# The sign word of the weight conversion: from a mask on VectorE to an add and a subtract on GpSimd

## The chip, the cores and the metric

The kernel runs on one core of a Trainium2 chip. The metric is the device time of one execution in microseconds (us); lower is better. The engines are named as in the profile: PE is TensorE (its weight loads are PEld), DVE is VectorE, ACT is ScalarE, POOL is GpSimd, SP issues most DMAs. Each engine works through its own list of instructions in order and waits for the others by semaphores.

## The reference

Eight batches of a two-way attention read are followed by a feed-forward block:

```python
def _attn_ref(x, state):              # x: 8 x 8 x 512 x 64, state: 8 x 8 x 32 x 64
    scores = scale * np.matmul(x, state.transpose(0, 1, 3, 2))
    a = softmax(scores); xread = np.matmul(a, state)
    scores2 = scale * np.matmul(state, x.transpose(0, 1, 3, 2))
    a2 = softmax(scores2); sread = np.matmul(a2, x)
    return np.concatenate([xread, sread], axis=2)

def _moe_ref(x, w_in, w_out):         # 4608 rows of 512; w_in 512 x 2048, w_out 2048 x 512
    h = x @ w_in
    g = h - np.tanh(h)
    return g @ w_out
```

(The softmaxes subtract the maximum and add 1e-9 to the sum.) `w_in` and `w_out` arrive as 8-byte numbers (float64), and the kernel makes 4-byte ones of them on the chip.

## The kernel before, in words

**Tiling.** The rows of the feed-forward block are cut into chunks: chunks 0 to 7 are the 512 x rows of one batch each, chunk 8 the state rows of all. `Chunk.hidden(f)` makes a 128 x 512 block of `h` in PSUM (tile `hps`), `Chunk.finish` (L523) takes tanh of it on ACT (tile `t`), subtracts on DVE, and splits the result into a high part (a cast on ACT) and a low part (a subtraction on DVE); `split` at L104 to L106 does this for every operand, so L106 is both a cast on ACT and a TENSOR_TENSOR on DVE. `Chunk.output(f)` multiplies the parts with the split rows of `w_out` (tiles `wo`) into `ops`. A product of two split operands is three matmuls (L515 to L517, L575 to L577). A batch's attention (`attention`, L313) leaves the tile `aT` (its two halves split at L393), which the chunk's first `hidden` needs.

**Weight conversion.** `Weight.steps` turns one 128 x 512 block of 8-byte numbers (tile `raw`, named `w..d` or `wo..d`) into 4-byte ones in four steps: L138 shifts the high words left by 3 and masks off two bits; L139 masks sign and top exponent bit out of the topmost 16-bit word into every second 16-bit element of a tile `r` (names `w..r`, `wo..r`, pool tag `c2` with four buffers); L140 on ACT scales the low words into the other elements; L141 adds the two as integers. There are 32 such blocks: `w00` to `w33` of `w_in`, `wo0` to `wo15` of `w_out`. A row of `w_out` is then split into `wo` by L106.

**Stages.** A start-up written out by hand (`SEQ`, L802) converts `w00` to `w03`, `wo0`, `wo1`, computes batch 0's attention and the first hidden blocks; in it, `a` to `p` with a number are the four conversion steps of a block. Then chunk 0's first eight blocks, chunk 1, the rest of chunk 0, chunks 2 and 3, and two pairs of chunks (class `Pair`) follow; the conversions of the other 26 blocks lie in chunk 0 and the first half of chunk 1, ahead of about 105 us.

**What sets the order.** Outside `SEQ` the instructions of each engine are put in order when the program is built: a scheduler goes by its own estimates of durations, by priorities and by `issue_after` gates. `convert` (L144) returns one step's instruction to such gates (`turn`), so that a conversion is issued behind the one before. The order is then fixed: an engine that waits at an instruction does nothing of what stands behind it. `m_first_two` (L163) multiplies converted `w_in` blocks by the state (PSUM tiles `mps`, L187); `free` (L202) copies these on ACT (L207).

Of the kernel before, what the change touches and what calls it, by code (L numbers as in the profile page):

```python
# [13 lines left out]
U16 = mybir.dt.uint16  # L14
ALU = mybir.AluOpType
# [16 lines left out]
LONE = 1  # L32
HALT = 8
PLAIN = (0, 1, 7)
TURN = ((0, 1, 2, 3), (1, 0, 3, 2))


@with_exitstack
def attention_ffn(ctx: ExitStack, tc: tile.TileContext, xT, xn, bd, bh, sp, sm, sl, win, wout, xout, tout, sout):
# [10 lines left out]
    nc = tc.nc  # L50
# [57 lines left out]
    class Weight:  # L108
# [17 lines left out]
        def steps(self, dst):  # L126

            if self.src.dtype == F32:
                return [lambda: None] * 3 + [lambda: nc.gpsimd.tensor_copy(dst, self.raw)]
            low, high = self.raw[:, :, 0], self.raw[:, :, 1]  # L130
            u, i = dst.bitcast(U32), dst.bitcast(I32)


            r = pool.tile([P, 512, 2], U16, tag="c2", name=f"{self.name}r", bufs=CSB)
            rest, top = r[:, :, 0], r[:, :, 1]
            return [

                lambda: nc.vector.tensor_scalar(u, high, 3, 0x3FFFFFFF, ALU.logical_shift_left, ALU.bitwise_and),  # L138
                lambda: nc.vector.tensor_single_scalar(top, self.raw.bitcast(U16)[:, :, 3], 0xC000, ALU.bitwise_and),  # L139
                lambda: nc.scalar.activation(rest, low, AF.Copy, scale=2.0**-29),  # L140
                lambda: nc.vector.tensor_add(i, i, r.rearrange("p f w -> p (f w)").bitcast(I32)),  # L141
            ]

        def convert(self, dst):  # L144
            return [step() for step in self.steps(dst)][1].ins


    m_first = {}
# [147 lines left out]
    def convert_wout(f, part):  # L296
        if f in PLAIN:
            if f // 2 not in plain:
                plain[f // 2] = big(f"wp{f}", [P, 2, DM], F32)
            return part.convert(plain[f // 2][:, f % 2])  # L300
        w = pool.tile([P, 512], F32, tag="c2", name=f"wor{f}", bufs=CSB)
        made = part.convert(w)
        wo[f] = big(f"wo{f}", [P, 2, DM], F32R)
        low = split(wo[f][:, 0], wo[f][:, 1], w)[1].ins
        return low if f in (2, 3) else made
# [7 lines left out]
    def attention(b, aT):  # L313
# [22 lines left out]
        def all_scores():  # L336
# [3 lines left out]
            for j in (2, 0, 3, 1):  # L340
                at = TURN[b][j] if b < 2 else j
                for hf in (1, 0):
# [68 lines left out]
    def state_read(b, ss):  # L411
# [40 lines left out]
        for hf in range(2):  # L452
            for k in range(4):
                for c in range(4):
                    cs = slice(32 * c, 32 * c + 32)
                    j = TURN[b][c] if b < 2 else c
                    with ExitStack() as behind:
# [11 lines left out]
        for hf in range(2):  # L469
            for j in range(4):  # L470
                h = 4 * hf + (TURN[b][j] if b < 2 else j)
                js = slice(32 * j, 32 * j + 32)
# [18 lines left out]
    class Chunk:  # L491
# [31 lines left out]
        def finish(self, f, ps):  # L523
            i, n = self.i, self.n
            t = pool.tile([P, 512], F32, tag="t", name=f"t{i}_{f}", bufs=TB)[:, :n]
            if CL <= i < B:
# [4 lines left out]
                return  # L531
            if i == 0 and f in PLAIN:
                g = self.g[f] = pool.tile([P, 512], F32, tag="g", name=f"g{i}_{f}", bufs=GB)
# [33 lines left out]
        def add(self, f, t):  # L567
            g, o = self.g[f], self.o[t]
            tok = slice(t * P, t * P + P)
            stop = f + 1 in self.begins or f == NFF - 1 or (self.i == B and t == 1 and f == NFF - 3)  # L570
            if self.i == 0 and f in PLAIN:
                w = plain[f // 2][:, f % 2]
# [81 lines left out]
    SPLITS = [8,9,10]  # L654
    split_it = iter(PLAIN)
    PAIRS = [1, 1, 9, 9, 11, 11, 13, 13, 15, 15]
# [556 lines left out]
```

## Time and profile before

| | |
|---|---|
| median of 3 runs | 637.64 us (637.53 to 640.27) |
| span of the profiled execution | 635.4 us (2.2 us less than the median) |
| PE busy | 627.7 us, 99% of the span |
| DVE busy | 474.8 us, 75% |
| ACT busy | 380.3 us, 60% |
| POOL busy | 24.0 us, 4%, nearly all of it DMA issue after 527 us |
| granted PE clock | 1.00, that is 2.4 GHz, in every stretch shown |

The page gives the profiled execution's time as its span alone; what a run takes beyond it lies around the kernel. PE's busy time includes the modelled tails of its matmuls, so it doesn't show by itself that PE always works; the start times of the matmuls do (three of a split product start 0.23 us apart, one of two 4-byte operands takes 0.86 us).

### The profile page before, as it was taken

What the parts mean: (1) busy time and instruction counts of PE and PEld (TensorE: products, weight loads), DVE (VectorE), ACT (ScalarE), POOL (GpSimd) and SP (SyncE); (2) the same over time, 40 slices, a digit from 0 to 9 for tenths busy, and PEclk for the clock granted to TensorE, in tenths of its full rate; (3) what the DMA queues carried; (4) which work ended last, traced back from release to release, by engine and by line L of the source; (5) the groups of instructions that cost most, each with busy time, mean ns of one, the idle gap of its engine ahead of it and who ended that gap; (6) DMA issues with size and microseconds to landing.
All of it is one profiled execution on the core that took longest, in us unless ns stands there. A gap on an engine that the chain in (4) does not pass through costs nothing.

```text
span 635.4 us, 9664 instructions
## 1 busy us (share of the span) xinstructions
PE 627.7 (99%) x3490; PEld 489.2 (77%) x3490; DVE 474.8 (75%) x770; ACT 380.3 (60%) x656; POOL 24.0 (4%) x38
## 2 busy tenths in 40 slices
PE   7999999999999999999999999999999999999997
PEld 4456677777777788778888788788888888888996
DVE  5999997686667956999445889989955789754542
ACT  5777777567666757676554675637565554533432
POOL 0000000000000000000000000000000001233200
PEclk9999999999999999999999999999999999999999
DMA  9993866568879856679952644765555537999700
GB/s 319 361 387 132 297 226 183 187 190 254 261 239 294 271 198 219 217 268 346 364 189 87 206 144 141 230 226 163 169 178 181 172 100 239 299 338 329 252 1 33
DMA packets 67439, 141.21 MB, mean 222 GB/s; under 512 B 6976, under 2 KB 28736, under 8 KB 67392
## 3 DMA queue, kind: packets, MB, share of 16 engines
q1 hardware_dynamic: 64544, 131.95, 63.4%
q0 software_dynamic: 2560, 8.39, 4.0%
q8 instruction: 27, 0.44, 0.3%
q10 hardware_dynamic: 288, 0.26, 0.1%
q14 instruction: 20, 0.16, 0.1%
HBM read 96.01 MB, written 44.56 MB: 221 GB/s over the span
## 4 chain that ended last, share of the span: by engine, by line
PE 94%; DVE 3%; ACT 2%; DMA 1%; issue 0%; ACTq 0%
PE X L1048 14%; PE hps L515 10%; PE hps L516 10%; PE hps L517 10%; PE ops L575 10%; PE ops L576 9%; PE ops L577 9%; PE Y0m L1048 5%; PE Y1m L1048 5%; PE mps L242 2%; PE mls L249 2%; PE ops L573 2%; PE rps L461 1%; PE pps L440 1%; PE hps L789 1%; PE mps L187 1%
## 5 line engine op out<-in xcount | busy, mean ns | idle before, releaser
L575 PE MATMUL ops<-wo,g 128*128 128x512 f32 x244 | 96.2, 400 | 0.0
L576 PE MATMUL ops<-wo,g 128*128 128x512 f32 x244 | 95.5, 391 | 0.0
L515 PE MATMUL hps<-aT,m 128*128 128x512 f32 x240 | 94.4, 395 | 0.0
L516 PE MATMUL hps<-aT,m 128*128 128x512 f32 x240 | 93.8, 391 | 0.1
L517 PE MATMUL hps<-aT,m 128*128 128x512 f32 x240 | 93.4, 390 | 0.0
L577 PE MATMUL ops<-wo,g 128*128 128x512 f32 x244 | 88.4, 396 | 0.0
L536 DVE TENSOR_TENSOR t<-hps,t 128x512 f32<-128x512 f32 (+1 forms) x77 | 48.7, 633 | 45.2 <-ACT t L536 44.8
L530 ACT ACTIVATE t<-hps 128x512 f32<-128x512 f32 x64 | 38.4, 599 | 66.3 <-PE hps L517 66.0
L536 ACT ACTIVATE t<-hps 128x512 f32<-128x512 f32 (+1 forms) x77 | 42.5, 552 | 56.7 <-PE hps L517 56.1
L530 DVE TENSOR_TENSOR G<-hps,t 128x512 f32<-128x512 f32 x64 | 43.9, 687 | 28.9 <-ACT t L530 28.7
L106 DVE TENSOR_TENSOR g<-t,g 128x512 fp32r<-128x512 f32 (+1 forms) x77 | 48.5, 632 | 16.1 <-ACT g L106 15.2
L575 PEld LDWEIGHTS ops<-wo,g 128*128 128x128 f32 x244 | 45.6, 188 | 17.4 <-ACT t L536 2.3
L106 ACT CAST g<-t 128x512 fp32r<-128x512 f32 (+1 forms) x77 | 44.3, 576 | 23.2 <-DVE t L536 22.8
L577 PEld LDWEIGHTS ops<-wo,g 128*128 128x128 f32 x244 | 45.5, 188 | 12.6 <-issue 2.5
L515 PEld LDWEIGHTS hps<-aT,m 128*128 128x128 f32 x240 | 45.1, 188 | 12.4 <-issue 2.0
L576 PEld LDWEIGHTS ops<-wo,g 128*128 128x128 f32 x244 | 45.8, 188 | 10.5 <-issue 1.1
L516 PEld LDWEIGHTS hps<-aT,m 128*128 128x128 f32 x240 | 45.1, 188 | 9.9 <-DVE aT L106 0.5
L517 PEld LDWEIGHTS hps<-aT,m 128*128 128x128 f32 x240 | 45.0, 188 | 9.4
L1048 PE MATMUL X<-g0m,W0m 128*128 128x512 f32 x192 | 47.8, 389 | 0.0
L1048 PE MATMUL X<-g1m,W1m 128*128 128x512 f32 x192 | 45.8, 389 | 0.0
L106 ACT CAST g1m<-G 128x1024 fp32r<-128x1024 f32 x28 | 29.2, 1054 | 27.0 <-PE X L1048 9.9
L1086 POOL DMA_DIRECT2D wl<-wod x32 | 23.3, 728 | 574.2 <-DMA wn<-wf 526.6
(275 smaller groups left out, 1134.5 us busy)
## 6 DMA issues: line engine op xcount, KB each, us to landing
mr<-md SPq DMA_DIRECT2D x26, 512.0 KB, 4.3
xT<-in_xT SPq DMA_DIRECT2D x16, 512.0 KB, 6.1
md<-st SPq DMA_DIRECT2D x64, 128.0 KB, 3.1
xn<-in_xn SPq DMA_DIRECT2D x16, 512.0 KB, 5.6
wsd<-ws SPq DMA_DIRECT2D x16, 512.0 KB, 4.7
wod<-wo SPq DMA_DIRECT2D x32, 256.0 KB, 7.3
W0m<-wsd SPq DMA_DIRECT2D x16, 512.0 KB, 3.6
W1m<-wsd SPq DMA_DIRECT2D x16, 512.0 KB, 4.7
```

The costliest lines, as they stand in the source:

```text
L106: return nc.scalar.copy(hi, src), (sub or nc.vector).tensor_sub(lo, src, hi)
L242: made = nc.tensor.matmul(pss[e], s0[rows, x, 2 * p + e], t[rows, y], start=(n == 0), stop=(n == 2))
L515: nc.tensor.matmul(ps, mhi[k][:, cols], ahi[:, k], start=(k == 0), stop=False)
L516: nc.tensor.matmul(ps, mhi[k][:, cols], alo[:, k], start=False, stop=False)
L517: made = nc.tensor.matmul(ps, mlo[k][:, cols], ahi[:, k], start=False, stop=(k == nk - 1))
L530: main(nc.scalar.activation(t, ps, AF.Tanh), nc.vector.tensor_sub(g, ps, t))
L536: tanhs.append((nc.scalar.activation(t, ps, AF.Tanh).ins, nc.vector.tensor_sub(t, ps, t).ins))
L575: nc.tensor.matmul(o, g[:, 0, tok], w[:, 0], start=(f in self.begins), stop=False)
L576: nc.tensor.matmul(o, g[:, 0, tok], w[:, 1], start=False, stop=False)
L577: return nc.tensor.matmul(o, g[:, 1, tok], w[:, 0], start=False, stop=stop).ins
L1048: made = nc.tensor.matmul(out[t], w[:, e, x, cols], y[:, e], start=first and j == 0 and e == 0 and c == 0, stop=last and j == 3 and e == 1 ...
L1086: nc.gpsimd.dma_start(wo[f][:, :, cols].bitcast(F32), wod[:, f % 2, half, f // 2])
```

## The change

The mask step leaves DVE. GpSimd reads the same 16-bit words, adds 1.5 * 2^37 to each and subtracts it again, which rounds the word to a multiple of 2^14, and writes it as 16 bits. The shift on DVE loses its mask: the two bits it leaves cancel in the integer add against the rounded word. `convert` now returns the shift, which is the first step, since the second is no longer on DVE.

```diff
@@ -32,6 +32,7 @@
 PLAIN = (0, 1, 7)
+COARSE = 1.5 * 2.0**37
 TURN = ((0, 1, 2, 3), (1, 0, 3, 2))
@@ -135,14 +136,14 @@
             return [
-                lambda: nc.vector.tensor_scalar(u, high, 3, 0x3FFFFFFF, ALU.logical_shift_left, ALU.bitwise_and),
-                lambda: nc.vector.tensor_single_scalar(top, self.raw.bitcast(U16)[:, :, 3], 0xC000, ALU.bitwise_and),
+                lambda: nc.vector.tensor_single_scalar(u, high, 3, ALU.logical_shift_left),
+                lambda: nc.gpsimd.tensor_scalar(top, self.raw.bitcast(U16)[:, :, 3], COARSE, COARSE, ALU.add, ALU.subtract),
                 lambda: nc.scalar.activation(rest, low, AF.Copy, scale=2.0**-29),
                 lambda: nc.vector.tensor_add(i, i, r.rearrange("p f w -> p (f w)").bitcast(I32)),
             ]
         def convert(self, dst):
-            return [step() for step in self.steps(dst)][1].ins
+            return [step() for step in self.steps(dst)][0].ins
```

Every line of the changed kernel behind L34 has a number higher by one. The scheduler, which knows other estimates for POOL than for DVE, also puts other instructions in another order. Two places matter below. The first is ACT's list where row 3 of `w_out` is split (`wor_404` is the converted row, `wo_410` its split; `mps_388` and `mps_389` are the second pair of state products). Before:

```order
L140 ACTIVATE wo3r<-wo3d 128x512
L207 COPY mr_312<-mps_322 128x512
L106 CAST m_561<-mr_187 128x1024
L207 COPY mr_313<-mps_323 128x512
L106 CAST wo_410<-wor_404 128x512
L140 ACTIVATE wo4r<-wo4d 128x512
L140 ACTIVATE wo5r<-wo5d 128x512
L207 COPY mr_312<-mps_388 128x512
```

And now:

```order
L208 COPY mr_312<-mps_322 128x512
L107 CAST m_561<-mr_187 128x1024
L141 ACTIVATE wo3r<-wo3d 128x512
L208 COPY mr_313<-mps_323 128x512
L208 COPY mr_312<-mps_388 128x512
L208 COPY mr_313<-mps_389 128x512
L107 CAST wo_410<-wor_404 128x512
L537 ACTIVATE t_4_418<-hps_4_415 128x512
```

The cast of `wo_410` has moved behind the copies of `mps_388` and `mps_389`. The second place is DVE's list from the low part of that split on. Before:

```order
L106 TENSOR_TENSOR wo_410<-wor_404,wo_410 128x512
L138 TENSOR_SCALAR wor_461<-wo4d 128x512
L139 TENSOR_SCALAR wo4r<-wo4d 128x512
L138 TENSOR_SCALAR wor_502<-wo5d 128x512
L139 TENSOR_SCALAR wo5r<-wo5d 128x512
L141 ISA wor_461<-wor_461,wo4r 128x1024
L141 ISA wor_502<-wor_502,wo5r 128x1024
L138 TENSOR_SCALAR wor_543<-wo6d 128x512
L139 TENSOR_SCALAR wo6r<-wo6d 128x512
L106 TENSOR_TENSOR wo_467<-wor_461,wo_467 128x512
L106 TENSOR_TENSOR wo_508<-wor_502,wo_508 128x512
```

And now:

```order
L107 TENSOR_TENSOR wo_410<-wor_404,wo_410 128x512
L139 TENSOR_SCALAR wor_461<-wo4d 128x512
L139 TENSOR_SCALAR wor_502<-wo5d 128x512
L537 TENSOR_TENSOR t_4_418<-hps_4_415,t_4_418 128x512
L537 TENSOR_TENSOR t_5_475<-hps_5_472,t_5_475 128x512
L107 TENSOR_TENSOR g_4_421<-t_4_418,g_4_421 128x512
L142 ISA wor_461<-wor_461,wo4r 128x1024
L376 STREAM_TRANSPOSE e_437<-s_434 128x512
L376 STREAM_TRANSPOSE e_443<-s_434 128x512
L139 TENSOR_SCALAR wor_543<-wo6d 128x512
```

The masks are gone, and the sums and splits of rows 4 and 5 now stand among the work on `t_4`, `t_5` and the attention of batch 1. From the low part of `wo_410` to the low part of `aT`'s first half, DVE's list holds the same instructions in both but for the masks of `wo4` to `wo7`.

## Rows read from the trace of the kernel before

**Rows 1.** Page: span, then busy us, share of span and instructions
```profile
span 635.4 us, 9664 instructions
...
PE 627.7 (99%) x3490; PEld 489.2 (77%) x3490; DVE 474.8 (75%) x770; ACT 380.3 (60%) x656; POOL 24.0 (4%) x38
```
**Rows 2.** Windows: stretch, us, busy of each engine (instructions), clock, DMA
```profile
19.09:105.00 85.91, 85.83 (x406) 54.96 (x406) 84.45 (x164) 65.34 (x112) 0.00 (x0) 1.00 0.75 266
35.08:54.62 19.54, 19.54 (x95) 11.86 (x94) 19.50 (x41) 12.94 (x23) 0.00 (x0) 1.00 0.71 271
105.00:635.40 530.40, 526.96 (x3002) 425.13 (x2998) 378.41 (x581) 303.50 (x524) 23.29 (x32) 1.00 0.66 211
```
**Rows 3.** Waits of PE: for whom, us in total, times, longest
```profile
PE mps L773 <- DVE w L141: 1.5, 2, 0.9
PE warm L701 <- DVE blank L73: 1.2, 1, 1.2
PE tps L716 <- ACT s L710: 0.8, 1, 0.8
PE aps L739 <- DVE e L734: 0.4, 1, 0.4
PE sps L705 <- DMA bdr<-in_bd: 0.2, 1, 0.2
```
**Rows 4.** Windows of L139 alone on DVE: stretch, us, busy (instructions)
```profile
0.00:110.00 110.00, 14.72 (x32) 1.00 0.78 275
35.08:54.62 19.54, 1.90 (x4) 1.00 0.71 271
...
20.00:55.00 35.00, 4.67 (x10) 1.00 0.82 305
55.00:110.00 55.00, 7.44 (x16) 1.00 0.70 234
```
**Rows 5.** Timeline, DVE: start, duration, instruction; back to back
```profile
30.45 0.47 DVE L139 TENSOR_SCALAR w12r<-w12d 128x512 uint16<-128x512 uint16 x1
30.79 0.42 DVE L138 TENSOR_SCALAR w<-w13d 128x512 uint32<-128x512 uint32 x1
31.12 0.46 DVE L139 TENSOR_SCALAR w13r<-w13d 128x512 uint16<-128x512 uint16 x1
...
47.38 0.70 DVE L378 TENSOR_TENSOR e<-e,m 128x512 f32<-128x512 f32 x1
47.98 0.70 DVE L536 TENSOR_TENSOR t<-hps,t 128x512 f32<-128x512 f32 x1
```
**Rows 6.** Timeline of the start-up: start, duration, instruction [idle before]
```profile
6.49 0.46 DVE L139 TENSOR_SCALAR w00r<-w00d 128x512 uint16<-128x512 uint16 x1 [5.35 <-DMA w00d<-in_win]
...
9.07 0.68 DVE L141 CUSTOM_DVE_ANT_0 w<-w,w00r 128x1024 uint16<-128x1024 uint16 x1
...
12.11 1.09 PE L773 MATMUL mps<-w,sps 128*64 128x128 f32 x16 [0.61 <-DVE w L141]
...
12.98 0.78 ACT L140 ACTIVATE w03r<-w03d 128x512 uint16<-128x512 uint32 x1 [0.70 <-DMA w03d<-in_win]
```
**Rows 7.** Timeline, 34 to 42 us: the split of row 3 and the copies
```profile
34.07 0.62 ACT L106 CAST wo<-wor 128x512 fp32r<-128x512 f32 x1 [0.49 <-DVE wor L141]
...
35.08 0.70 DVE L106 TENSOR_TENSOR wo<-wor,wo 128x512 fp32r<-128x512 f32 x1
...
36.11 1.09 PE L187 MATMUL mps<-w,sps 64*32 64x512 f32 x16
...
37.24 0.59 ACT L207 COPY mr<-mps 128x512 f32<-128x512 f32 x1 [0.64 <-PE mps L187]
...
37.77 1.22 ACT L106 CAST wo<-wor 128x512 fp32r<-128x512 f32 x2
...
39.37 0.79 ACT L140 ACTIVATE wo6r<-wo6d 128x512 uint16<-128x512 uint32 x1
40.02 0.79 ACT L140 ACTIVATE wo7r<-wo7d 128x512 uint16<-128x512 uint32 x1
```
**Rows 8.** Timeline, 54 to 56 us: aT's low part and PE
```profile
54.62 1.46 DVE L106 TENSOR_TENSOR aT<-at,aT 128x512 fp32r<-128x512 f32 x2
...
54.62 0.61 PE L515 MATMUL hps<-aT,m 128*128 128x512 f32 x2
55.32 0.50 PE L516 MATMUL hps<-aT,m 128*128 128x512 f32 x1
```
**Rows 9.** Groups of POOL instructions: busy, mean ns, idle before
```profile
masks.py:199 POOL TENSOR_SCALAR_AFFINE_SELECT ident<-ident 128x128 f32<-128x128 f32 x1 | 0.3, 287 | 0.1
masks.py:197 POOL MEMSET ident<- 128x128 f32 x1 | 0.2, 204 | 0.3 <-POOLq L1198 0.3
...
L1198 POOL MEMSET const-float32-0.0<- 128x1 f32 x1 | 0.1, 93 | 0.2 <-issue 0.2
```

## The prediction

> **What bounds the kernel now.** I read the page's busy shares first: PE is busy for 627.7 of 635.4 us [rows 1]. Since a busy PE need not be a fed one, I looked at stretches next: from 19.09 us to 105 us it lacks 0.08 us of 85.91, and from 105 us on 3.4 us of 530.4 [rows 2]. PE's own waits add up to 4.1 us, and all of them lie in the start-up, before 19 us [rows 3]. So from 19 us on the kernel is one stream of matmuls, at full clock. Nothing that makes another engine faster can shorten that stream. A change can win only what PE waits in the start-up, and it loses whatever time PE is newly left without work.
>
> DVE is the other engine to watch: until 105 us it is busy for 84.45 of 85.91 us [rows 2], so PE is fed just in time. Where it is closest shows at 55 us: chunk 1's first matmuls with the high part of `aT` start at 54.62, 0.23 us apart, the next needs the low part, which DVE makes from 54.62 to 55.31, and it starts at 55.32 [rows 8]. PE has nothing else to do there. The path to the end runs through DVE's making of `aT`, without slack.
>
> **What leaves DVE, and what that is worth.** There are 32 masks, all before 110 us [rows 4]. Back to back, a mask starts 0.34 us before the next instruction [rows 5], so DVE loses 32 x 0.335 = 10.7 us of work. The shift keeps its price: the same one instruction with one operation fewer, and 0.335 us is what mask and shift, with one and two operations, both take.
>
> In the start-up, two PE waits can shrink. The second `mps` product waits 0.61 us for a conversion [rows 6], with one mask ahead of its sum that goes: -0.335. The transposes `aps` wait 0.4 us [rows 3] behind a second mask: at most -0.37 more. Not all of it arrives, since ACT has to copy `aps` and stands at `w03r` until that block lands at 12.98 [rows 6]. I take -0.5 us, with 0 and -0.7 as ends. The other 26 masks bring nothing by themselves, because PE doesn't wait there. On SP the stores of converted blocks and the loads for batches 1 and 2 change places in nine lines; the only DMA that PE waits for is the first, 0.2 us [rows 3], so I cost this at nothing; the cover is that the loads are issued well ahead of their use.
>
> **What is added on POOL.** POOL does nothing in this stretch [rows 2]. Its trace shows no instruction like the new one, so I bound it. A memset takes 93 ns for one column and 204 ns for 128, the select, which reads and writes, 287 ns [rows 9]; stretched in a straight line to 512 columns that is an estimate of 0.54 us and 0.87 us. The new one reads and writes like the select, but builds no pattern: I take 0.7 us, between the two. The queue holds 32 x 0.7 = 22 us in 100. In the start-up the word of `w00` is due at 9.07 and can start at 6.49 [rows 6], 2.6 us for an instruction of 0.7: hidden under DVE's other work. Cover would be gone above 2.6 us each. POOL's DMAs all come after 105 us [rows 2], behind the last new instruction.
>
> **What moves: a new wait at row 3 of `w_out`.** This is the term that I expect to decide the sign. Before, ACT's cast of `wo_410` starts at 34.07 and DVE's low part at 35.08 [rows 7], while the product pair `mps_388`, `mps_389` runs on PE only at 36.11 and its first copy on ACT at 37.24 [rows 7]. In the new order ACT makes this cast behind both copies. PE gets to the pair by its stream, 0.5 us earlier by the start-up's gain. So: first copy at 37.24 - 0.5 = 36.74; copies and casts follow at 0.53 us (37.24 to 37.77), so the second copy starts at 37.27 and the cast at 37.80; it takes 0.62 and ends at 38.42. DVE's low part, due in its list, waits for it, idle, and starts at 38.45 rather than 35.08. Queued behind it on DVE is everything up to `aT`.
>
> Between these two points DVE worked 19.54 us without a pause (19.50 busy) [rows 2]. The list is the same but for four masks [rows 4], 1.34 us: 18.2 us. One more wait appears: DVE reaches `g_4`'s low part after the low part, two shifts and two 0.60 us subtractions [rows 5], at 38.45 + 0.6 + 0.67 + 1.2 = 40.92, but ACT has, from 38.33, two tanh (0.5 each), two conversions (0.65 each, 39.37 to 40.02 [rows 7]) and the cast (0.62): 41.25. That is 0.3 us. `aT`'s low part then starts at 38.45 + 18.2 + 0.3 = 57.0, where it started at 54.62 [rows 8]: +2.4 us, all on PE, since its stream has no other work. The four masks and the start-up's 0.5 us are inside this sum.
>
> **The price of POOL beside DVE.** The masks of `wo5`, `wo6`, `wo7`, `w20`, `w21` run on POOL in that stretch, while DVE is the path. If the two engines don't disturb each other this costs 0. If DVE had to stand still during each, it costs 5 x 0.7 = 3.5 us (5 x 0.87 = 4.4 at the long end). No row shows the two at once on tiles in SBUF. I take a middle value: in 18.2 us DVE has four shifts (1.34 us) and 15 instructions of 0.60 us with both operands in SBUF (splits, integer sums, the subtraction and scaling of `e`), 10.3 us or 57%; if those alone exclude POOL, five instructions cost 0.57 x 3.5 = 2.0 us. After 57 us there are 14 more; DVE is relieved of 16 masks [rows 4], 5.4 us, there, and delayed by at most 14 x 0.7 x 0.57 = 5.6: nothing, with +4.4 as the end (14 x 0.7 - 5.4).
>
> The Trainium skill speaks against the change here: SBUF — State Buffer, section "SBUF: two separate sides", says that VectorE and GpSimd share one pair of ports, held exclusively for a whole instruction, and that a VectorE instruction with two SBUF inputs collides with a GpSimd one that reads SBUF. No row of this kernel shows it; by that rule the 2.0 us fall due, without it the sum stops at +2.4. GPSIMD Engine Reference, section "Engine selection", calls one-input work on GpSimd roughly line-rate: an estimate of 512 / 1.2 GHz = 0.43 us for an instruction, which would make the same term 1.2 us.
>
> **Sum.** +2.4 (new wait, net of all gains) + 2.0 (POOL beside DVE) = +4.4 on the profiled execution's 635.4 us, so 639.8; with the 2.2 us by which the runs' median stands above this span, 642.0 us.
>
> **Rivals.** *The order alone.* POOL doesn't hinder DVE: +2.4, 640.0 us. For it: nothing in the trace shows a collision. Against: most of what DVE does there reads two tiles of SBUF.
>
> *Not slower.* DVE gets its 3.35 us (the ten masks between 20 and 55 us [rows 4]) and `aT` comes no later than PE asks for it; the start-up's gain stays: -0.5, 637.1 us. The mechanism is that ACT doesn't stand at the copies: if the pair of products came to PE 2.4 us or more earlier than at 36.11, the cast would be done by 36 and the saved masks would cover the rest. For it: DVE is the path there and loses work. Against: PE's stream before the pair has no gap [rows 2], so the pair can't come earlier than the start-up allows.
>
> *POOL heavier.* 0.87 us an instruction, DVE standing still for each: 2.4 + 4.4 = 6.8, and after 57 us DVE falls behind by 14 x 0.87 - 5.4 = 6.8 us, of which I let a third reach PE, 2.2: +9.0, 646.6 us. For it: DVE has no spare time until 105 us. Against: such a price needs both ends at once.
>
> That the change doesn't do what it says I leave out; the masks are gone from DVE's list.
>
> **How the numbers follow.** Chances: forecast 0.42, with a range of its own of 640.6 to 643.8; order alone 0.27; not slower 0.13; POOL heavier 0.18. The range for 8 in 10 goes from 638.2, just above the third case, to 646.5: what is left out is most of that case and the upper half of the last. About 0.5%, 3.2 us, is what a measurement here can tell from no change. Above 640.8 lie nearly all of the forecast (0.40), a little of the order alone (0.03) and the heavy case (0.17): slower 0.60. Within: 0.37. Faster by 3.2 us isn't in reach, as the start-up holds 4.1 us of waits and the change touches 1.0 of them [rows 3]: 0.03 for error.
>
> **What would show it.** In the profile after: POOL with 32 TENSOR_SCALAR of 0.5 to 0.9 us; DVE idle for about 3 us ahead of a split of `wo` at 35 to 38 us, released by ACT; PE with a wait of 2 us or more for `aT` near 57 us, where no wait was; no PE wait to speak of after 110 us. The port term shows as longer spacing than 0.60 us, or idle time without a releaser, on DVE between 38 and 58 us: 2 us in all if right, none if the rival is. I am wrong if `aT` comes by 55 us, if PE waits elsewhere (at `wo4` to `wo6` for instance) for longer than for `aT`, or if the start-up gets longer because POOL's words come late.

## The result, and the profile after

The changed kernel takes 642.98 us (median of 6 runs, 642.09 to 645.06), the kernel before 637.39 us beside it: a ratio of 1.0085, with a 95% interval of 1.0071 to 1.0098. It is 5.6 us slower; 642.0 us had been forecast. The profiled execution has a span of 641.1 us, 5.7 more than before [rows 1]. The page's span, then busy us, share and instructions:

```profile
span 641.1 us, 9713 instructions
...
PE 628.9 (98%) x3490; PEld 489.3 (76%) x3490; DVE 473.5 (74%) x738; ACT 380.3 (59%) x656; POOL 98.2 (15%) x70
```

DVE has 32 instructions fewer but is hardly less busy: 1.3 us less, where 10.7 us of masks went. POOL gained 32 instructions and 74 us, that is 2.3 us each. PE's waits (for whom, us in total, times, longest):

```profile
PE mps L774 <- DVE w L142: 2.8, 2, 1.8
PE hps L516 <- ACT aT L107: 1.5, 1, 1.5
...
PE ops L577 <- DVE wo L107: 0.9, 1, 0.9
...
PE hps L514 <- ACT mr L208: 0.7, 1, 0.7
PE mps L765 <- DVE w L142: 0.5, 1, 0.5
```

Against [rows 3], the wait for `mps` has grown by 1.3 us, one of 0.5 is new and the 0.4 us for `aps` is gone: that is the start-up. The other three are new and lie between 39 and 61 us. All of PE's waits add up to 8.8 us, where they were 4.1; PE's busy time, which counts the modelled tails of the matmuls, has grown by 1.2 us with the same 3490 matmuls. The start-up, in order of time (start, duration, instruction, idle time before it and what ended it):

```profile
6.66 2.34 POOL L140 TENSOR_SCALAR w00r<-w00d 128x512 uint16<-128x512 uint16 x1 [5.35 <-DMA w00d<-in_win]
...
10.13 2.14 POOL L140 TENSOR_SCALAR w01r<-w01d 128x512 uint16<-128x512 uint16 x1 [1.13 <-DMA w01d<-in_win]
...
12.19 2.27 POOL L140 TENSOR_SCALAR w02r<-w02d 128x512 uint16<-128x512 uint16 x1
12.31 1.09 DVE L142 CUSTOM_DVE_ANT_0 w<-w,w01r 128x1024 uint16<-128x1024 uint16 x1 [1.11 <-POOL w01r L140]
...
13.45 1.09 PE L774 MATMUL mps<-w,sps 128*64 128x128 f32 x16 [1.78 <-DVE w L142]
```

Before, the sum of `w01` stood here:

```profile
11.36 0.69 DVE L141 CUSTOM_DVE_ANT_0 w<-w,w01r 128x1024 uint16<-128x1024 uint16 x1
```

POOL begins the word of `w01` when the block lands, at 10.13, and takes 2.14 us. DVE waits 1.11 us for it, and the sum itself, which begins just behind the start of POOL's next word, takes 1.09 us where before a sum took 0.68 [rows 6]. The second product starts at 13.45 instead of 12.11 [rows 6], 1.34 us later: 0.95 for the late start of the sum (12.31 and 11.36), 0.4 for its length.

The place at row 3 of `w_out`:

```profile
36.16 1.88 PE L514 MATMUL hps<-at,mr 128*128 128x512 f32 x4
...
37.97 1.09 PE L188 MATMUL mps<-w,sps 64*32 64x512 f32 x16
39.10 1.07 ACT L208 COPY mr<-mps 128x512 f32<-128x512 f32 x2 [3.05 <-PE mps L188]
...
40.06 0.63 ACT L107 CAST wo<-wor 128x512 fp32r<-128x512 f32 x1
...
40.73 0.69 DVE L107 TENSOR_TENSOR wo<-wor,wo 128x512 fp32r<-128x512 f32 x1 [3.33 <-ACT wo L107]
```

Here stands what the prediction said: ACT waits 3.05 us for PE's pair of products, copies both tiles, and only then makes the cast, so DVE stands idle for 3.33 us. The matmul at 36.16 is the one that stood at 34.30 [rows 7]; it and the pair (36.11 before) are both 1.86 us late, which is what the start-up lost in these two profiles. Then `aT`, and the stretches of DVE's way to it and of the rest (columns as in [rows 2]):

```profile
60.34 1.29 DVE L107 TENSOR_TENSOR aT<-at,aT 128x512 fp32r<-128x512 f32 x2
60.36 0.73 PE L516 MATMUL hps<-aT,m 128*128 128x512 f32 x2 [1.49 <-ACT aT L107]
...
63.49 3.59 PE L574 MATMUL ops<-wp,g 128*128 128x512 f32 x8
```
```profile
40.73:60.34 19.61, 17.19 (x75) 10.56 (x73) 19.43 (x36) 12.73 (x23) 13.02 (x6) 1.00 0.54 183
...
110.00:641.10 531.10, 527.37 (x3004) 425.41 (x3002) 379.08 (x583) 303.74 (x524) 23.40 (x32) 1.00 0.65 212
```

DVE's low part of `aT` starts at 60.34 instead of 54.62 [rows 8], 5.72 us late, and the end is 5.7 us late: after `aT` nothing is lost or won in sum. DVE needs 19.61 us for the same way that took 19.54 [rows 2], though four masks of 1.34 us are gone. So the 5.72 us are 1.86 (start-up), 3.79 (row 3: low part at 40.73 where 35.08 + 1.86 = 36.94 would have kept pace) and 0.07 (the way to `aT`).

### The profile page after: what moved, and what is told of

The parts are those of the page before. It is cut to its first block, busy times and chain, and to the rows that moved or that the text cites. A ratio compares the mean times of both kernels' runs of the same rounds, so it can differ in the third digit from the quotient of the medians.

```text
span 641.1 us, 9713 instructions
## 1 busy us (share of the span) xinstructions
PE 628.9 (98%) x3490; PEld 489.3 (76%) x3490; DVE 473.5 (74%) x738; ACT 380.3 (59%) x656; POOL 98.2 (15%) x70
## 4 chain that ended last, share of the span: by engine, by line
PE 91%; DVE 3%; DMA 2%; ACT 1%; POOL 1%; issue 1%; SPq 0%; ACTq 0%
PE X L1049 14%; PE hps L516 10%; PE hps L517 10%; PE hps L518 10%; PE ops L576 9%; PE ops L578 9%; PE ops L577 9%; PE Y0m L1049 5%; PE Y1m L1049 5%; PE mps L243 2%; PE mls L250 2%; PE ops L574 2%; DMA w01d<-in_win 1%; PE rps L462 1%; PE hps L790 1%; PE pps L441 1%
```

## The experiments

The three causes are the six words of the start-up on POOL, the other 26 on POOL, and the late cast at row 3. They were switched one by one; the scheduler still moves other instructions when a part of the words is on POOL, so that a run can change more than its one cause (start_dve below). Who makes a word is chosen by the block's name:

```diff
+            self.pool = name not in ('w00', 'w01', 'w02', 'w03', 'wo0', 'wo1')
...
-                lambda: nc.gpsimd.tensor_scalar(top, ...
+                (lambda: nc.gpsimd.tensor_scalar(top, ...)) if self.pool
+                else (lambda: nc.vector.tensor_single_scalar(top, ..., 0xC000, ALU.bitwise_and)),
```

(the shift keeps its mask wherever DVE makes the word). With either part on DVE the scheduler puts row 3's cast ahead of the copies again; where it was to stay late, the cast and the low part of row 3 were gated:

```diff
+        with ExitStack() as behind:
+            if f == 3:
+                behind.enter_context(tc.issue_after(freed[0]))
-        low = split(wo[f][:, 0], wo[f][:, 1], w)[1].ins
+            low = split(wo[f][:, 0], wo[f][:, 1], w)[1].ins
```

Single profiles differ by up to 1.1 us in the start-up even where nothing in it was changed, so the last two columns read each trace from one point on: the start of the `hps` matmul that stood at 34.30 us before [rows 7], and the time from there to DVE's low part of `aT`. The start-up's differences begin ahead of the conversion: DVE's sum of `w00` starts at 9.07 us before, at 9.25 in the change, and between 8.93 and 9.88 in the kernels that make this block's word on DVE.

| kernel | start-up words | other 26 | cast of row 3 | median / before, us | ratio, 95% interval | `hps` at | to `aT` |
|---|---|---|---|---|---|---|---|
| before | DVE | DVE | early | | | 34.30 | 20.32 |
| start_pool | POOL | DVE | early | 638.99 / 637.72 | 1.0021 [1.0010, 1.0032] | 35.93 | 20.46 |
| start_dve | DVE | POOL | early | 639.19 / 637.72 | 1.0024 [1.0007, 1.0041] | 34.79 | 22.09 |
| cast_late | DVE | DVE | late | 642.30 / 637.72 | 1.0071 [1.0053, 1.0089] | 34.83 | 24.13 |
| start_dve_late | DVE | POOL | late | 641.53 / 637.29 | 1.0069 [1.0057, 1.0082] | 35.39 | 24.15 |
| start_pool_late | POOL | DVE | late | 644.63 / 637.29 | 1.0117 [1.0103, 1.0131] | 36.65 | 24.14 |
| changed | POOL | POOL | late | 642.98 / 637.39 | 1.0085 [1.0071, 1.0098] | 36.16 | 24.18 |

**start_pool.** 

> Only the six blocks of the start-up have their word made by POOL; the other 26 keep mask and masked shift on DVE, and ACT's and DVE's lists at row 3 are those of before. Theory: the words of w01 and w02 come late, since an instruction takes 2.1 us and can't start before the block lands, and PE waits for the two sums: first hidden matmul at 36.2 us where before had 34.30, and nothing is given back, since PE's stream has no gap after it: +1.9 us, 639.3 us (638.8 to 639.8). Rival (the start-up's loss comes from the order or is made up while DVE has slack up to 28 us): within 0.5 us of before, 637.4. Rival (the prediction's step): -0.5 us, 636.9.

PE's second product and the `hps` matmul:

```profile
13.42 1.09 PE L779 MATMUL mps<-w,sps 128*64 128x128 f32 x16 [1.44 <-DVE w L147]
...
35.93 1.88 PE L519 MATMUL hps<-at,mr 128*128 128x512 f32 x4
```

The same late product as in the change, and the loss reaches the `hps` matmul, 1.6 us late; from there to `aT` it goes as before (20.46). About 0.5 of the 1.6 us were there already at the sum of `w00`, at 9.56 instead of 9.07, which waited for no word. The runs say 1.3 us (0.0021 x 637.5, interval 0.6 to 2.0). The start-up's loss is real and nothing gives it back; the prediction's gain of 0.5 us falls.

**start_dve.** 

> The six blocks of the written-out start-up (w00 to w03, wo0, wo1) keep the mask and the masked shift on DVE; the other 26 words are made by POOL as in the change. The scheduler then puts ACT's cast of row 3 of w_out ahead of the second pair's copies again, as in the kernel before. Theory (the change's 5.7 us are 1.9 us of late words in the start-up, about 2.7 us of the wait at row 3, about 1.2 us of POOL beside DVE): the first hidden matmul is back at 34.3 us (36.16 with the whole change), DVE's low part of row 3 at about 35.1 us without idle time of 3 us ahead of it, and of the 1.2 us most is paid by the four masks that DVE is rid of on the way to aT: 0 to +1 us against before, 638.0 us (637.2 to 638.6). Rival 1 (words of 2.05 us are late all along, the start-up is not special): +3 us or more, 640.5. Rival 2 (POOL beside DVE costs the 2.0 us or more that the prediction took, and the masks pay none of it): +2 us, 639.4.

DVE's timeline:

```profile
30.89 1.00 DVE L140 TENSOR_SCALAR w<-w13d 128x512 uint32<-128x512 uint32 x1
31.82 0.86 DVE L140 TENSOR_SCALAR wor<-wo3d 128x512 uint32<-128x512 uint32 x1
...
33.80 1.21 DVE L107 TENSOR_TENSOR m<-mr,m 128x1024 fp32r<-128x1024 f32 x1
34.93 1.13 DVE L147 CUSTOM_DVE_ANT_0 wor<-wor,wo3r 128x1024 uint16<-128x1024 uint16 x1
36.75 0.69 DVE L107 TENSOR_TENSOR wo<-wor,wo 128x512 fp32r<-128x512 f32 x1 [0.68 <-ACT wo L107]
```

The idle time of 3 us is gone and the time is still 1.5 us above before (0.4 to 2.6). I had 0 to 1 us; the second rival's 2 us is as near. DVE's instructions are longer here and there: shifts of 1.00 and 0.86 us where before one took 0.42 [rows 5], a sum of 1.13 instead of 0.68. But the 1.77 us that the way from the `hps` matmul to `aT` is longer are not POOL's collisions alone. DVE's low part of row 3 starts 1.96 us behind the `hps` matmul instead of 0.78: in this list the low part of `m` (33.80) stands ahead of the sum of row 3 (34.93) and no longer behind it, so that ACT's cast comes late and DVE waits 0.68 us. From there to `aT` DVE takes 20.13 us for what took 19.54, with four masks fewer. So with POOL beside DVE more is lost than the masks bring, in part by collisions and in part by the changed order; this run does not separate the two.

**cast_late.** 

> The kernel before with all masks on DVE and nothing on POOL; only the cast and the low part of row 3 of w_out are issued behind the copies of the second pair of state products, as the change's order has them, and DVE's list behind it has the subtraction on t_4 ahead of the sums, much as in the change. Theory (the order at row 3 by itself costs what DVE waits there): first copy at 37.24 us as before, cast at 38.3, DVE's low part at 38.9 after some 3 us of idle time, then 19.5 us of work: aT's low part at 58 to 58.8 us where before had 54.62, so +3.2 to +4.2 us, 641.1 us. That is more than the 2.7 us that I put down to it in the change, since here DVE keeps its four masks. Rival (DVE catches up, or PE has other work until aT comes): +1 us or less, 638.4. The start-up stays: first hidden matmul at 34.3 us.

ACT and DVE, in order of time:

```profile
37.76 1.07 ACT L207 COPY mr<-mps 128x512 f32<-128x512 f32 x2 [3.66 <-PE mps L187]
38.72 0.63 ACT L106 CAST wo<-wor 128x512 fp32r<-128x512 f32 x1
...
39.38 0.69 DVE L106 TENSOR_TENSOR wo<-wor,wo 128x512 fp32r<-128x512 f32 x1 [3.69 <-ACT wo L106]
...
58.96 1.29 DVE L106 TENSOR_TENSOR aT<-at,aT 128x512 fp32r<-128x512 f32 x2
```

With not one instruction on POOL, the late cast costs 4.5 us (3.4 to 5.7), a little more than the 3.2 to 4.2 expected: the idle time, the low part 1.62 us behind the first copy, and `aT` 24.13 us behind the `hps` matmul, as in the change (24.18). Of this 3.81 us stand at `aT` (24.13 - 20.32); the other 0.8 us of the profile are lost behind it, where PE waits 0.94 us for a copy on ACT at 171.79. From the low part to `aT` DVE takes 19.58 us, as before, so the idle time is the whole loss on this way: the low part starts 4.6 us behind the `hps` matmul in all four kernels with the late cast, and 0.78 before and in start_pool. The wait at row 3 is shown, and so is that PE has nothing else to do until `aT` comes.

**start_dve_late.** 

> The six blocks of the start-up keep their masks on DVE, the other 26 words are on POOL, and the cast and low part of row 3 are issued behind the copies of the second pair: the change without its start-up. Theory (order at row 3 and start-up add up, and on the way from row 3 to aT the four masks that DVE is rid of, 1.3 us, are taken back by POOL's collisions with it, 0.2 us for each of five or six words): DVE's low part of row 3 at 39.4 us as in the kernel with the late cast alone, aT's low part at 58.9 us, so +4.3 us against before less some noise: 641.8 us (641.0 to 642.4). Rival 1 (the masks pay and POOL costs nothing): aT at 57.6, 640.5. Rival 2 (the start-up's loss is hidden in the wait at row 3, so that nothing is won by mending it): as the whole change, 643.0.

As the theory had it: 4.4 us above before, 24.15 us to `aT`. With the late cast it makes no difference whether DVE has the four masks (24.13) or POOL has the words (24.15): the 1.34 us that the masks bring and what POOL's instructions take from DVE come out equal. Against start_dve, the late cast costs 2.9 us here (0.0069 - 0.0024 = 0.0045).

**start_pool_late.** 

> Only the six blocks of the start-up have their word made by POOL, the other 26 keep their masks on DVE, and the cast and low part of row 3 are issued behind the copies of the second pair: start-up and order without any POOL instruction behind 21 us. Theory (they add up): second pair's first copy at 39.1 us, DVE's low part of row 3 at 40.7, aT's low part 19.6 us later at 60.3 as in the whole change: +5.5 us, 643.2 us (642.4 to 643.8). Rival (the start-up's delay is taken up by the wait at row 3): as the late cast alone, 642.0 or less. Rival 2 (POOL beside DVE between 38 and 58 us is a part of the change's loss that nothing else pays): 1.3 us less than the whole change, 641.7.

24.14 us to `aT`, so the second rival falls here too, and the start-up's loss adds to the late cast's. The time is 1.4 us above the theory's all the same. TensorE's granted clock has the reason (columns: stretch, us, PE busy, clock, DMA):

```profile
58.00:61.00 3.00, 0.18 (x1) 1.00 0.00 0
62.00:65.00 3.00, 3.00 (x9) 0.50 0.38 93
66.00:70.00 4.00, 4.00 (x13) 1.00 0.95 324
```
```profile
60.81 0.73 PE L524 MATMUL hps<-aT,m 128*128 128x512 f32 x2 [3.04 <-ACT aT L107]
...
65.52 3.59 PE L582 MATMUL ops<-wp,g 128*128 128x512 f32 x8
```

PE waited 3.04 us for `aT` in one piece; behind that its clock was at 0.50, the lower level of 1.2 GHz, for about 3 us. From the first matmul with `aT` to the next product (`ops<-wp`) PE takes 4.71 us, where the change, at full clock, takes 3.13 (60.36 to 63.49): 1.6 us for the clock. All four runs of this kernel list a mean clock of 0.994 to 0.997. In the change's profiled run PE's waits are in pieces of 0.7, 0.9 and 1.5 us and the clock stays at 1.00; of its six runs one, the longest (645.06 us), lists 0.994.

**cast_first.** 

> The whole change, but the copies of the second pair are issued behind the cast of row 3 of w_out; the rest of the lists stays much as in the change (the tanh on t_4 still stands behind both copies, and DVE has the subtraction on t_4 ahead of the sums of rows 4 and 5). Theory A (the cast is only the first of a row of things that stand behind the copies): DVE's low part moves to about 38 us, the idle time of 3 us moves behind it, to the subtraction on t_4 at about 42 us, and aT comes only 0.5 us earlier, at 59.8: 642.4 us (641.9 to 642.8). Theory B (the place of the cast alone costs the 2.8 us): low part at 38 us, 19.6 us to aT, which comes at 57.6: 640.3 us (639.8 to 641.0).

```diff
+        if (q, p) == (1, 3):
+            held.extend((lambda o=o, i=i: free(o, i)) for o, i in zip((m_first[q][:, k], m_second[q][:, k]), pss))
+            return
...
+            if st == 2:
+                with tc.issue_after(cast3[0]):
+                    for x in held:
+                        x()
```

DVE's timeline, TensorE's clock as above, and PE:

```profile
38.47 0.69 DVE L107 TENSOR_TENSOR wo<-wor,wo 128x512 fp32r<-128x512 f32 x1 [0.69 <-ACT wo L107]
...
42.32 0.69 DVE L543 TENSOR_TENSOR t<-hps,t 128x512 f32<-128x512 f32 x1 [1.45 <-ACT t L543]
...
60.18 1.29 DVE L107 TENSOR_TENSOR aT<-at,aT 128x512 fp32r<-128x512 f32 x2
```
```profile
60.00:63.00 3.00, 2.80 (x7) 0.50 0.04 8
```
```profile
60.20 1.22 PE L522 MATMUL hps<-aT,m 128*128 128x512 f32 x2 [2.96 <-ACT aT L107]
...
64.51 3.60 PE L580 MATMUL ops<-wp,g 128*128 128x512 f32 x8
```

The low part comes 2.3 us earlier than in the change, and next to nothing is won: from the `hps` matmul (36.53) to `aT` 23.65 us, 0.53 less than in the change. The idle time has moved to `t_4`, whose tanh ACT makes behind the copies and two conversions. So theory A holds, and the late cast is only the first of several instructions that stand too late; before, DVE converted rows 4 to 6 in this stretch. The time, 643.55 us (1.0098, 1.0083 to 1.0113), is no better than the change's because the clock fell to 0.50 here too, behind a wait of 2.96 us: PE takes 4.31 us from the first matmul with `aT` to the next product instead of 3.13, 1.2 us more. All four runs of this kernel list a mean clock of 0.996 or 0.997.

**pool_beside.** 

> The kernel before, every mask on DVE and every list the same; added are nine instructions on POOL of the change's form (512 16-bit words in steps of 8 bytes, add and subtract, 16-bit out in steps of 4 bytes) on two tiles that nobody else uses, released by the low part of row 2 of w_out at about 30 us, so that they run back to back until about 49 us, while DVE is the path to aT. No other engine waits for them. Theory (a short collision at an instruction's start or end, 0.2 us of DVE's time for each): nine times 0.2 = +1.8 us, aT's low part at 56.4 us, 639.2 us (638.5 to 639.9). Rival 1 (VectorE work with two operands in SBUF stands still for the whole of a POOL instruction): nine times 2.05 us times 57% = +10.5 us, 647.9. Rival 2 (no collision; the longer DVE instructions in the change come from something else, such as DMA): 637.4, within 0.4 us of before. The Trainium skill, SBUF — State Buffer, section 'SBUF: two separate sides', states the first rival's mechanism.

```diff
+        nc.gpsimd.tensor_copy(word[:, 1:2], gate)
...
+        for _ in range(9):
+            nc.gpsimd.tensor_scalar(top[:, :, 1], word[:, :, 3], COARSE, COARSE, ALU.add, ALU.subtract)
```

POOL's two rows, and four of DVE's:

```profile
30.48 11.20 POOL L316 COPY word<-wo 128x1 f32<-128x1 f32 x1 [28.28 <-DVE wo L107]
41.78 20.76 POOL L319 TENSOR_SCALAR top<-word 128x512 uint16<-128x512 uint16 x9
```
```profile
44.10 1.09 DVE L107 TENSOR_TENSOR g<-t,g 128x512 fp32r<-128x512 f32 x1
...
46.33 1.04 DVE L107 TENSOR_TENSOR g<-t,g 128x512 fp32r<-128x512 f32 x1
...
48.49 1.08 DVE L390 TENSOR_TENSOR e<-e,m 128x512 f32<-128x512 f32 x1
...
51.29 0.68 DVE L107 TENSOR_TENSOR g<-t,g 128x512 fp32r<-128x512 f32 x1
```

The nine began late, at 41.78 us, because the one-element copy that released them took 11.2 us. They start at 41.78, 43.98, 46.20, 48.37, 50.58 and so on, about 2.2 us apart. DVE's instructions at 44.10, 46.33 and 48.49, which begin some 0.12 us behind such a start, take 0.4 us longer than the 0.68 of the same kind in the middle of a POOL instruction (51.29). A reduction that begins 0.11 us behind a start, at 50.69, takes its usual 0.67 us. Seven of the nine start ahead of `aT`, which comes 21.63 us behind the `hps` matmul instead of 20.32: 0.2 us each. In all the runs lost 2.7 us (1.0043, interval 1.0027 to 1.0059), 0.3 us for each of the nine. The short collision holds, a little above its size. The Trainium skill, SBUF — State Buffer, section "SBUF: two separate sides", says that the pair of ports is held exclusively for a whole instruction; this trace doesn't agree, since a VectorE instruction with two operands in SBUF takes its 0.68 us while POOL's runs on.

**pool_forms.** 

> The kernel before with fifteen instructions of 512 elements a partition added on POOL, on tiles of their own, three of each form: 16-bit words in steps of 8 bytes with add and subtract (the change's), the same with the add alone, 16-bit words side by side with both, 4-byte floats side by side with both, the same with the add alone. Read here is the time of one on POOL. Theory (512 elements at some 4 ns each, whatever the form, so that a count of elements sets the price): 2.0 to 2.1 us for all five. Rival 1 (steps and 16 bits are what is slow): the floats side by side at 1 us or less, the strided ones at 2.05. Rival 2 (each operation is a pass): 1.0 to 1.1 us for the forms with the add alone.

POOL's five groups of three, in the order of the expectation:

```profile
41.51 6.49 POOL L319 TENSOR_SCALAR top<-word 128x512 uint16<-128x512 uint16 x3
48.08 5.72 POOL L321 TENSOR_SCALAR top<-word 128x512 uint16<-128x512 uint16 x3
53.89 6.45 POOL L323 TENSOR_SCALAR top<-word 128x512 uint16<-128x512 uint16 x3
60.42 7.06 POOL L325 TENSOR_SCALAR top<-word 128x512 f32<-128x512 f32 x3
67.57 5.56 POOL L327 TENSOR_SCALAR top<-word 128x512 f32<-128x512 f32 x3
```

2.16, 1.91, 2.15, 2.35 and 1.85 us each: neither steps nor 16 bits make it slow, and the second operation costs 0.25 to 0.5 us. If the count of elements sets most of the price, 512 of them cost some 3.7 ns each; no other count was run, so that is not shown. (One run, 641.66 us.)

**three_pool.** 

> Only w03, wo0 and wo1 have their word made by POOL, the three of the start-up whose words of 2.1 us can be there before they are asked for; the other 29 keep their masks on DVE, and the order at row 3 is that of before. Theory: the second product doesn't wait longer than before (0.61 us), the wait for the second transposes (0.4 us) shrinks, each of three POOL words costs DVE 0.2 us, and aT is as near to its limit as before: -0.4 to +0.3 us against before, within what can be measured. Rival (any word on POOL in the start-up comes late): first hidden matmul later than before's 34.3 us by 0.5 us or more, +0.5 to +1.5 us.

```profile
12.99 2.22 POOL L143 TENSOR_SCALAR w03r<-w03d 128x512 uint16<-128x512 uint16 x1 [11.68 <-DMA w03d<-in_win]
```
```profile
13.12 0.93 DVE L145 TENSOR_SCALAR w02r<-w02d 128x512 uint16<-128x512 uint16 x1
```
```profile
14.77 0.63 PE L745 MATMUL aps<-ident,e 128*128 128x128 f32 x4 [0.85 <-DVE e L740]
```

638.29 us beside 637.81 (1.0013, interval 1.0001 to 1.0026): 0.8 us more (0.1 to 1.7), no gain, and between the two theories. The `hps` matmul stands at 35.47, 1.17 us later than before, which is the rival's sign; but 0.7 us of that were there at the sum of `w00` (9.79), whose mask DVE makes here. No word is late, but the mask of `w02` runs into the start of POOL's word of `w03` and takes 0.93 us instead of 0.45, and the transposes that stand behind it wait 0.85 us instead of 0.4 [rows 3]. One collision on the path undoes three masks. None of these kernels beats the kernel before.

## Why the prediction was right, and where it was not

**What bounds the kernel** held: `aT` came 5.72 us late and the end 5.7. The one wait of 2 us or more for `aT` that was to show it came in pieces, 0.7 us for `mr`, 0.9 for `wo` and 1.5 for `aT`: 3.1 of the 3.9 us by which `aT` is later than the start-up alone makes it.

**The new wait at row 3** was the main term and was right, place and size. From ACT's first copy to DVE's low part I had 1.71 us (36.74 to 38.45), the trace has 1.63 (39.10 to 40.73), and DVE's idle time is 3.33 us. cast_late shows it without POOL. What the prediction did not see is that the cast is not the only thing that stands behind the copies (cast_first).

**The start-up** was wrong in sign: -0.5 us forecast, +1.86 in the profile, and this is the largest miss. (By start_pool's runs it is 1.3 us, 0.6 to 2.0; the size hangs on the profile that it is taken from, the sign does not.) The step that failed is "hidden under DVE's other work": it was checked for `w00`, whose word had 2.6 us, and its price of 0.7 us left room. The word takes 2.1 to 2.3 us. For `w00` that still just fits (6.66 to 9.00; the sum starts at 9.25); for `w01`, which lands at 10.13 and whose sum stood at 11.36 before, the room was 1.2 us, and I did not look.

**The price of an instruction on POOL** was mis-sized by a factor of three: 0.54 and 0.87 us, the ends drawn from memset and select in a straight line, did not hold 2.1. By the Trainium skill's "roughly line-rate" (GPSIMD Engine Reference, section "Engine selection") the estimate was 0.43 us; pool_forms disagrees with it for all five forms.

**POOL beside DVE**: 2.0 us and a wait of 0.3 on an 18.2 us way made 20.5; the trace has 19.61, so 1.4 us in place of 2.3. Two errors worked against each other: the instructions are three times as long as assumed, and six start on this way and not five, but they stop DVE for 0.2 to 0.3 us each and not for 57% of their length. After `aT` I took nothing, and there is nothing.

So 4.3 us for `aT` were forecast (4.4 in the prediction's rounded sum) and 5.72 came: +2.36 from the start-up's term, -0.08 at row 3, -0.89 on the way to `aT`. The forecast case, slower, was right, and by the right main term. That its time is only 1 us off is in part luck: two misses of opposite sign, +2.36 and -0.89, stood beside that term. Of the rivals, the order alone (640.0) lacked the start-up; "POOL heavier" named the right price tag and the wrong effect: the instruction is heavier still, but DVE doesn't stand still for it. What I had written as a sign of error, a start-up that gets longer because the words come late, is what the profile shows.

What stays open: why a collision costs up to 0.4 us and only near the start of POOL's instruction, and which instructions of DVE are exempt. The share of the start-up in the change's 5.6 us is known to no better than about 0.7 us, by the interval of start_pool.

## What to carry to other kernels

Taking work off a busy engine won nothing here, where the end hangs on a chain through several engines; look at what the scheduler does to the other engines' lists, since one cast behind two copies, with what then stood behind it, cost 4.5 us here, more than the 1.0 us of PE's waits that 32 masks could touch. A cover has to be checked for each instance of a repeated step, above all for the one whose input lands last. And an operation that no trace shows is to be priced with an upper end as far off as the argument can bear: here a factor of three in one price was harmless in one place and turned a sign in another.

## What the runs showed of the hardware

- An elementwise instruction of 128 x 512 on POOL took 1.85 to 2.35 us (means of three, pool_forms) whether 16 or 32 bits, in steps or side by side, with one operation or two; single words of the changed kernel took 2.1 to 3.6 us.
- The first COPY on POOL, of one element a partition, took 11.2 us, in both kernels that had one (pool_beside, pool_forms); the first TENSOR_SCALAR of the changed kernel had no such time. Its cause was not tried.
- After PE had waited about 3.0 us in one piece its clock fell to 0.50 for some 3 us in cast_first and start_pool_late, at 1.2 and 1.6 us. In the profiled run of cast_late, with a wait of 3.02 us, it stayed at 1.00; three of that kernel's six runs list a mean clock of 0.997:

```profile
59.00:62.00 3.00, 3.00 (x12) 1.00 0.00 0
```
